# Sparse attention in units of two batches, with tiled scores and routing lists built on the chip

## The chip, the core and the metric

The kernel runs on one core of a Trainium2 chip. The core has a matrix engine (TensorE, PE in the profile; its weight loads are listed apart as PEld), a vector engine (VectorE, DVE), a scalar engine (ScalarE, ACT), a general engine (GpSimd, POOL) and a sequencer that mostly starts transfers (SyncE, SP). Each works through its own list of instructions in order and waits for the others on semaphores. Transfers between DRAM and the on-chip memory run on 16 DMA engines. TensorE writes to PSUM, a small memory of 8 banks; the other operands lie in SBUF.

The metric is the time of one execution on the device in microseconds (us).

## The reference

Block-sparse attention over 4 batches, 8 heads, 768 positions and 64 channels, and then a mixture of 8 experts, in which every token goes to at most one expert:

```python
mask = np.abs(blk_i - blk_j) <= 1
mask = mask | (blk_i == 0) | (blk_j == 0) | (blk_i == n_blocks - 1) | (blk_j == n_blocks - 1)
for qb in range(n_blocks):
    for kb in sampled_blocks[qb]:          # three per query block
        mask[qb * 32:(qb + 1) * 32, kb * 32:(kb + 1) * 32] = True
scores = np.where(mask, scale * q @ k.T, -1e9)
attn = softmax(scores); out = attn @ v     # (4, 8, 768, 64)
x = out as 3072 tokens of 512
do_compute = x @ w_skip > 0                # the others keep x
e_idx = argmax(x @ w_gate); gate = the softmax's value there
y = gate * (relu(x @ w1[e_idx]) @ w2[e_idx]); result = x + y
```

The 768 positions are 24 blocks of 32. Query blocks 0 and 23 look at all keys. Each of the other 22 looks at eight blocks of keys at most: blocks 0 and 23, its own and its two neighbours, and three sampled ones; so 256 keys.

## The kernel before, in words

The work has three stages in time.

**Dense units.** Query blocks 0 and 23 make 16 units (class `Dense`), one for each batch and pair of heads.

**Sparse units.** The other 22 query blocks make 88 units (class `Sparse`), one for each block and batch, in the order of the blocks. A unit has 8 heads of 32 queries, that is 256 rows of scores of 256 keys, and runs through six steps:

- `S`: scores on TensorE, four matmuls of 256 columns (L401). The channels of two heads lie one above the other in the 128 partitions. The queries of such a pair are laid out with zeros (64 columns: 32 of the one head with zeros in the lower half, 32 of the other with zeros in the upper half), so one matmul over all 128 partitions gives the scores of both heads. Two such matmuls go to different halves of the output's partitions.
- `M`: row maxima on VectorE (L409), and a second small instruction that scales and negates them (L410).
- `X`: exponentials on ScalarE, two of 256 columns (L416), with the score's scale in the instruction.
- `T`: four transposes of 128x128 on TensorE (L421).
- `V`: ScalarE copies the transposed 512 columns from PSUM to SBUF (L425).
- `A`: 16 matmuls of 65 columns on TensorE (L435), each on a strip of 32 of the array's columns, four strips in turn; the 65th column sums the row. `N` then divides on VectorE (L446, L447, L448).

An fp32 matmul is two records in the profile, a transpose one. The main loop (`for k in range(-LA, nu + 1)`) writes the steps of different units beside each other: in step k stand S and M of unit k+3, X of unit k+2, T of unit k+1, V and A of unit k, N of unit k-1. So TensorE's list is S, A, T, S, A, T without end.

The keys of a query block are gathered on the chip: `load_k` lets GpSimd copy them out of `kts`, which holds all keys, into `kg[0]` or `kg[1]` by the block's parity (two copies for the window, L187, and three for the sampled blocks, L202, as multiplications by a tile of ones). The values come by DMA from DRAM, five transfers of 260 KB for each block (`load_v`: two of the window, three sampled), and the queries in one of 512 KB (`load_q`). Key and value loads of block i+2 are issued behind the last unit of block i. Four transfers of 64 KB write a finished block to `out`.

**Routing lists.** After each group of three or four blocks (`BATCHES`), `route` works out which expert each token goes to and its place in that expert's list, in seven steps that the main loop takes one at a time (`fetch`). Its last act is a scatter by GpSimd, one per block: 128 entries of two numbers (token, gate) into the DRAM tensor `lst` (L73, out `lst`). `pick_first` and `look_first` choose, some units before the end, the expert with the most tokens so far, read its first 256 entries back from `lst`, and gather those tokens' rows.

**Experts.** If that first expert has its 256 tokens, its first matmuls (`gemm1` on `early["t"]`, L747 to L749) start at once behind the attention, and the routing of the last group is written between them (`beside`). Then `lists` reads all of `lst` by one transfer, `order_lists` puts the first expert in front, and eight experts follow, each with two matrix products in split precision. The weights of the first expert and half of those of the next (twelve transfers of 512 KB) overwrite `kts` when the last keys have been gathered.

## Time and profile before

| | |
|---|---|
| runs | 573.26, 575.48 (median), 579.07 us |
| the profiled execution | 573.99 us, span 572.3 us, granted TensorE clock 0.96 |
| TensorE busy | 499.7 us, 87% of the span |
| VectorE, ScalarE, GpSimd busy | 358.0, 250.8, 214.8 us |
| moved by DMA | 108.36 MB, 189 GB/s on average |
| first matmul of a sparse unit | at 56.74 us |
| first matmul of an expert | at 301.25 us |

The span is the time between the first and the last instruction. Busy time is the union of an engine's instructions. Several small matmuls can run in the array at once; their listed mean is the time of one from start to end, so mean times count is more than the busy time. "issue" stands where an engine waited for nothing that the profile shows. In the tables of stretches, the columns are the stretch, its length, the busy time and number of instructions of PE, PEld, DVE, ACT and POOL, then the granted clock, the share of time for which the DMA engines were busy, and GB/s.

### The profile page before, as it was taken

How to read it: one execution, taken by the hardware profiler on the slowest of the kernel's cores; microseconds unless marked ns; L12 is line 12 of the kernel's file. 1: busy time of each engine (PE TensorE's matmuls, PEld its weight loads, DVE VectorE, ACT ScalarE, POOL GpSimd, SP SyncE). 2: the span in 40 equal slices, each digit the busy share in tenths (PEclk: the TensorE clock that was granted, in tenths of full speed). 3: DMA queues.
4: the chain of work that ended last, by engine and by line, in shares of the span. 5: the costliest groups of instructions: out<-in, count | busy, mean ns of one | idle time of the engine just before them, and what ended most of it. 6: DMA issues, size and time to landing. Idle time of an engine off the chain costs nothing.

```text
span 572.3 us, 16047 instructions
## 1 busy us (share of the span) xinstructions
PE 499.7 (87%) x5842; PEld 369.4 (65%) x5842; DVE 358.0 (63%) x1028; ACT 250.8 (44%) x576; POOL 214.8 (38%) x236
## 2 busy tenths in 40 slices
PE   6999999899899799799877976989999977899980
PEld 4777765466566466465456755978797854777970
DVE  4877677678668578688667616656649573482510
ACT  3444555365355365454552205536354535361300
POOL 2008345736636636637436332150413240512020
PEclk9999999899799899999989979999999989999995
DMA  8999989967969879868996531564544564811010
GB/s 287 345 317 223 225 217 271 235 165 213 233 158 221 199 182 224 218 161 219 255 316 206 197 129 33 182 211 168 195 173 155 197 199 177 296 70 45 3 43 13
DMA packets 49565, 108.36 MB, mean 189 GB/s; under 512 B 7175, under 2 KB 35208, under 8 KB 43842
## 3 DMA queue, kind: packets, MB, share of 16 engines
q1 hardware_dynamic: 43760, 84.69, 53.9%
q0 software_dynamic: 5008, 20.69, 10.7%
q8 instruction: 70, 1.15, 1.0%
q14 instruction: 149, 1.22, 0.7%
q10 hardware_dynamic: 578, 0.61, 0.3%
HBM read 96.34 MB, written 12.30 MB: 190 GB/s over the span
## 4 chain that ended last, share of the span: by engine, by line
PE 43%; issue 27%; DVE 12%; DMA 8%; POOL 4%; SPq 1%; POOLq 1%; ACT 1%; DVEq 0%; ACTq 0%
PE sp L401 11%; PE op L435 7%; PE tp L421 7%; DMA x<-out,lt 6%; PE op L357 4%; PE sp L322 3%; DVE m L409 3%; DVE m L410 2%; PE tp L345 2%; POOL out L73 2%; POOL x L577 2%; DVE xs L448 1%; PE hp L749 1%; PE hp L747 1%; DMA kts<-kt 1%
## 5 line engine op out<-in xcount | busy, mean ns | idle before, releaser
L401 PE MATMUL sp<-kg,q 128*64 128x256 f32 x704 | 100.5, 405 | 1.6 <-issue 1.6
L425 ACT COPY pt<-tp 128x512 f32<-128x512 f32 x88 | 51.7, 587 | 107.5 <-PE tp L421 94.9
L409 DVE TENSOR_REDUCE m<-sp 128x2 f32<-128x512 f32 x88 | 60.2, 684 | 39.9 <-PE sp L401 32.1
L202 POOL TENSOR_TENSOR kg<-kts,onesf 128x512 f32<-128x512 f32 x66 | 82.1, 1274 | 0.1
L73 POOL DMA_INDIRECT out<-o,lt x17 | 18.8, 1104 | 153.7 <-DVE o L830 153.4
L187 POOL TENSOR_SCALAR kg<-kts 128x512 f32<-128x512 f32 x50 | 30.0, 621 | 121.4 <-PE sp L401 82.5
L416 ACT ACTIVATE pr<-sp,m 128x256 f32<-128x256 f32 x176 | 74.2, 478 | 2.8 <-DVE rs L446 2.8
L747 PE MATMUL hp<-xh,w1h 128*128 128x256 f32 (+3 forms) x192 | 59.5, 310 | 14.6 <-DVE o L830 7.5
L401 PEld LDWEIGHTS sp<-kg,q 128*64 128x64 f32 x704 | 44.9, 140 | 34.7 <-issue 22.1
L421 PE MATMUL tp<-ident,pr 128*128 128x128 f32 x352 | 60.4, 292 | 4.2 <-issue 4.1
L752 ACT ACTIVATE hh<-hp 128x256 fp32r<-128x256 f32 (+2 forms) x56 | 21.3, 383 | 85.7 <-PE hp L749 63.0
L748 PE MATMUL hp<-xl,w1h 128*128 128x256 f32 (+3 forms) x192 | 58.9, 307 | 0.0
L749 PE MATMUL hp<-xh,w1l 128*128 128x256 f32 (+3 forms) x192 | 58.8, 306 | 0.0
L435 PEld LDWEIGHTS op<-va,pt 128*32 128x32 f32 x1376 | 31.3, 110 | 42.4 <-ACT pt L425 23.2
L755 DVE SCALAR_TENSOR_TENSOR hl<-hp,hh 128x256 fp32r<-128x256 f32 (+2 forms) x56 | 23.2, 416 | 50.8 <-ACT hh L752 19.7
L435 PE MATMUL op<-va,pt 128*32 128x65 f32 x1376 | 48.3, 228 | 7.5 <-issue 2.2
L435 PE MATMUL op<-vb,pt 128*32 128x65 f32 x1376 | 49.0, 223 | 6.6 <-issue 6.6
L747 PEld LDWEIGHTS hp<-xh,w1h 128*128 128x128 f32 x192 | 37.3, 194 | 17.7 <-issue 15.4
L421 PEld LDWEIGHTS tp<-ident,pr 128*128 128x128 f32 x352 | 38.1, 143 | 12.8 <-issue 5.0
L813 PE MATMUL yp<-w2h,hh 128*128 128x512 f32 x112 | 45.4, 405 | 0.0
L814 PE MATMUL yp<-w2l,hh 128*128 128x512 f32 x112 | 45.0, 402 | 0.1
L815 PE MATMUL yp<-w2h,hl 128*128 128x512 f32 x112 | 44.7, 399 | 0.0
(209 smaller groups left out, 983.7 us busy)
## 6 DMA issues: line engine op xcount, KB each, us to landing
vb<-v SPq DMA_DIRECT2D x68, 260.0 KB
va<-v SPq DMA_DIRECT2D x48, 260.0 KB
kts<-w SPq DMA_DIRECT2D x6, 2048.0 KB
kts<-w POOLq DMA_DIRECT2D x6, 2048.0 KB
q<-qs SPq DMA_DIRECT2D x22, 512.0 KB
vt<-v SPq DMA_DIRECT2D x16, 390.0 KB
kts<-w SPq DMA_DIRECT2D x12, 512.0 KB
kts<-kt SPq DMA_DIRECT2D x15, 384.0 KB
```

Source lines behind the costliest of these rows:

```text
L202: nc.gpsimd.tensor_tensor(out=kg[x][:, :, c0:c0 + BS], in0=kts[:, :, bass.ds(kr * BS, BS)], in1=onesf[:, 0:BS].unsqueeze(1).broadcast_to([ ...
L401: nc.tensor.matmul(out=self.sp[64 * j:64 * j + 64, g, :], lhsT=qt[self.i][:, p, :], rhs=kg[self.x][:, p, :], start=True, stop=True)
L409: lambda: nc.vector.reduce_max(out=self.mx, in_=self.sp, axis=AX.X),
L416: nc.scalar.activation(out=self.pr[:, g, :], in_=self.sp[:, g, :], func=AF.Exp, bias=self.mx[:, g:g + 1], scale=SCALE)
L421: nc.tensor.transpose(out=self.tp[:, u, :], in_=self.pr[:, u // 2, (u % 2) * P:(u % 2) * P + P], identity=ident)
L425: nc.scalar.copy(out=self.pt, in_=self.tp)
L435: nc.tensor.matmul(out=self.op[32 * hh:32 * hh + 32, g, :], lhsT=self.pt[:, 2 * g + t, 32 * hh:32 * hh + 32], rhs=vt[:, 8 * self.b + 4 * g ...
L747: nc.tensor.matmul(out=hp[:, 0:w], lhsT=wh[:, f, k, :], rhs=xh[:, k, 0:w], start=(k == 0), stop=False)
L748: nc.tensor.matmul(out=hp[:, 0:w], lhsT=wh[:, f, k, :], rhs=xl[:, k, 0:w], start=False, stop=False)
L749: nc.tensor.matmul(out=hp[:, 0:w], lhsT=wl[:, f, k, :], rhs=xh[:, k, 0:w], start=False, stop=(k == NK1 - 1))
L813: nc.tensor.matmul(out=yp, lhsT=hh[:, f, cs], rhs=wh[:, f, :], start=(f == 0), stop=False)
L814: nc.tensor.matmul(out=yp, lhsT=hh[:, f, cs], rhs=wl[:, f, :], start=False, stop=False)
```

## The change

It touches the sparse stage and the lists; the dense units and the experts are as before but for the layout of heads and the places from which lists are read.

- **Units of two batches.** 44 sparse units in place of 88. A unit holds two batches' 512 rows: twice the exponentials, transposes, copies and value matmuls of a unit before.
- **Tiled scores.** Queries come without zeros (`qs` is half as large). A head's score matmul takes its 64 channels alone, in the upper or the lower half of the array's rows, and its 32 queries go to one strip of 32 columns. A unit has 16 such matmuls of 256 columns, the two heads of a pair in turn; heads of the upper half go to the PSUM tile `sp0`, those of the lower half to `sp1`.
- **The scale goes to the queries.** GpSimd multiplies each block's queries by 0.125 when they have landed; the reduction for the maxima negates, and the small instruction behind it is gone.
- **Keys copied plainly.** All copies are `tensor_copy`.
- **Two courses.** The blocks are taken in the order 1, 12, 2, 13, ... 11, 22 (`ORDER`); blocks 1 to 11 use the first store of keys and values, blocks 12 to 22 the second. Since a store sees neighbours one after another, only one new block of its window has to be fetched: one key copy in place of two, four value transfers in place of five.
- **Lists on the chip.** A token's place is turned into a row of 128 zeros and a one (`rows_of_ones`) and its two numbers into a row of 24 columns each (`entries`); a matmul of the two adds the group's tokens into a table in PSUM (`put`), and VectorE adds that to `lsf`. No scatter to `lst` and no reading back are left, outside a branch for experts of more than 384 tokens. `route` has 13 steps in place of 7, and the last group has four blocks in place of two.
- **Other places.** The loop counts in `q`, two for each sparse unit; the twelve weight loads are issued one at each q from 14 before the end (before: two, two, and then one at each step from 10 before the end). The filling of later rows of `out` is spread over eight small transfers.

The inner changes of the diff:

```diff
+ORDER = [i for pair in zip(range(1, HALF), range(HALF, NB - 1)) for i in pair]
+BATCHES = [[0, NB - 1] + ORDER[:2]] + [ORDER[a:b] for a, b in ((2, 6), (6, 9), (9, 12), (12, 15), (15, 18), (18, 22))]
...
     def window(i):
-        return (i - 1, i, i + 1) if i <= 2 else (i, i + 1)
+        return (i - 1, i, i + 1) if i in ORDER[:2] else (i + 1,)
...
         for r, c0 in enumerate((64, 96, 224)):
             kr = nc.gpsimd.value_load(kidx[0:1, i, r:r + 1], min_val=0, max_val=NB - 1)
-            nc.gpsimd.tensor_tensor(out=kg[x][:, :, c0:c0 + BS], in0=kts[:, :, bass.ds(kr * BS, BS)],
-                                    in1=onesf[:, 0:BS].unsqueeze(1).broadcast_to([P, NPAIR, BS]), op=ALU.mult)
+            nc.gpsimd.tensor_copy(out=kg[x][:, :, c0:c0 + BS], in_=kts[:, :, bass.ds(kr * BS, BS)])
+
+        nc.gpsimd.tensor_scalar(out=qt[i], in0=qt[i], scalar1=SCALE, scalar2=0.0, op0=ALU.mult, op1=ALU.add)
...
         def S(self):
-            self.sp = ps_s.tile([P, 2, 256], F32, name="sp")
+            self.sp = [ps_s.tile([P, 2, 256], F32, name=f"sp{w}") for w in range(2)]
             for g in range(2):
-                for j in range(2):
-                    p = 4 * b + 2 * g + j
-                    nc.tensor.matmul(out=self.sp[64 * j:64 * j + 64, g, :], lhsT=qt[self.i][:, p, :], rhs=kg[self.x][:, p, :], start=True, stop=True)
+                for a in range(4):
+                    p = 4 * (self.b + g) + a
+                    for w in range(2):
+                        ws = slice(64 * w, 64 * w + 64)
+                        nc.tensor.matmul(out=self.sp[w][32 * a:32 * a + 32, g], lhsT=qt[self.i][ws, p, :], rhs=kg[self.x][ws, p, :], start=True, stop=True)
...
         def M(self):
-                lambda: nc.vector.reduce_max(out=self.mx, in_=self.sp, axis=AX.X),
-                lambda: nc.vector.tensor_single_scalar(out=self.mx, in_=self.mx, scalar=-SCALE, op=ALU.mult),
+            return [lambda w=w: nc.vector.tensor_reduce(out=self.mx[:, w], in_=self.sp[w], axis=AX.X, op=ALU.max, negate=True) for w in range(2)]
...
-        def scatter():
-            for t in range(T):
-                scatter_to(
-                    out=lst[:, :], out_offset=bass.IndirectOffsetOnAxis(ap=st["adr"][:, t:t + 1], axis=0),
-                    in_=st["pay"][:, t, :], in_offset=None, bounds_check=P * E * LC - 1, oob_is_err=False)
+        def put():
+            st["lp"] = ps_r.tile([P, 2, E * CS], F32, name="rps")
+            for t in range(T):
+                nc.tensor.matmul(out=st["lp"], lhsT=st["plo"][:, t], rhs=st["phi"][:, t], start=(t == 0), stop=(t == T - 1))
+        d6 = [
+            lambda: V.tensor_tensor(out=lsf, in0=lsf, in1=st["lp"], op=ALU.add),
...
+    def sparse_step(k):
+        q = nd + 2 * (k - nd) if k >= nd else k
+        if fresh:
+            units[k + 2].S()
+        mix(units[k - 1].N(), [])
+        pe, soon, then, pool = work(q)
+        mix(soon, [])
+        if k + 1 < nu:
+            units[k + 1].T()
+            units[k + 1].V(0)
+        if pe is not None:
+            pe()
+        flush()
+        if k < nu:
+            units[k].A()
+        if fresh:
+            mix(units[k + 2].M(), [])
+        if k + 2 < nu:
+            units[k + 2].X()
+        if k + 1 < nu:
+            units[k + 1].V(1)
...
+            pe, soon, then, pool = work(q + 1)
```

TensorE's list in the middle of the sparse stage, before, from one unit's scores to the next unit's: sp are scores, op the products with the values va and vb, tp the transposes.

```order
L401 MATMUL sp<-kg_89,q 64x256 x4
L435 MATMUL op<-va_90,pt 32x65 x4
L435 MATMUL op<-vb_92,pt 32x65 x4
L435 MATMUL op<-va_90,pt 32x65 x4
L435 MATMUL op<-vb_92,pt 32x65 x4
L421 MATMUL tp<-ident,pr 128x128 x4
```

The same place in the changed kernel, from the last pair of a unit's scores (seven such pairs stand ahead of it):

```order
L429 MATMUL sp_1466<-kg_85,q 32x256
L429 MATMUL sp_1467<-kg_85,q 32x256
L449 MATMUL tp<-ident,pr 128x128 x8
L468 MATMUL op<-va_88,pt 32x65 x4
L468 MATMUL op<-vb_90,pt 32x65 x4
L468 MATMUL op<-va_88,pt 32x65 x4
L468 MATMUL op<-vb_90,pt 32x65 x4
```

Two more such pairs of op rows end the unit. Scores now come as 16 matmuls of 32 columns of queries in turn to two tiles; the transposes of the next unit have moved ahead of this unit's value products; and the array changes from one shape of work to another three times for two batches, where it did so six times.

GpSimd's list at a block's key gather before, where it follows a group's scatter:

```order
L73 DMA lst<-pay,adr 26624x2 x4
L187 TENSOR_SCALAR kg_89<-kts 128x16x32 x2
L201 TENSOR_LOAD kidx
L201 ISA x2
L202 ISA
L202 TENSOR_TENSOR kg_89<-kts,onesf 128x16x32
```

And in the changed kernel, behind the scaling of the block before:

```order
L214 TENSOR_SCALAR q<-q 128x512
L192 COPY kg_85<-kts 128x16x32
L211 TENSOR_LOAD kidx
L211 ISA x2
L212 ISA
L212 COPY kg_85<-kts 128x16x32
```

The last four rows of either piece stand three times for a block (once shown). The scatter is gone, the window takes one copy, and the scaling of the queries, which waits for their transfer, stands at the end of each gather.

VectorE's list between two units before: the maxima of one unit, then the division of another.

```order
L409 TENSOR_REDUCE m_2469<-sp 128x2
L410 TENSOR_SCALAR m_2469<-m_2469 128x2
L446 TENSOR_SCALAR rs<-op 128x2
L447 RECIPROCAL rs<-rs 128x2
L448 TENSOR_TENSOR xs<-op,rs 128x128
```

In the changed kernel, at a place where two steps of the list building stand between (col, phi and lsb are the rows of ones that `put` multiplies):

```order
L479 TENSOR_SCALAR rs<-op 128x4
L480 RECIPROCAL rs<-rs 128x4
L481 TENSOR_TENSOR xs<-op,rs 128x256
L315 TENSOR_TENSOR col<-cols,cols_of 128x96
L311 TENSOR_TENSOR phi<-col,pays 128x192
L436 TENSOR_REDUCE m_2327<-sp_2190 128x2
L436 TENSOR_REDUCE m_2327<-sp_2191 128x2
L307 TENSOR_TENSOR lsb<-pos,rows_of 128x512
```

The division comes once for two batches, the small instruction behind the maxima is gone, and steps of the lists stand ahead of a unit's maxima.

## The prediction

> **What bounds the kernel now.** I read the page first, then busy times by stretches: the sparse stage lies between the first scores of a sparse unit, at 56.74, and the first expert matmul, at 301.25.

> ```profile
> PE 499.7 (87%) x5842; PEld 369.4 (65%) x5842; DVE 358.0 (63%) x1028; ACT 250.8 (44%) x576; POOL 214.8 (38%) x236
> ...
> 56.74 1.08 PE L401 MATMUL sp<-kg,q 128*64 128x256 f32 x8
> 301.25 0.36 PE L747 MATMUL hp<-xeh,w1h 128*128 128x256 f32 x1 [0.36 <-DVE ohs L288]
> ...
> 20.00:40.00 20.00, 20.00 (x201) 15.24 (x199) 16.64 (x67) 8.48 (x19) 0.00 (x0) 1.00 1.09 334
> 60.00:292.00 232.00, 211.36 (x3876) 133.42 (x3876) 167.80 (x585) 119.69 (x274) 124.22 (x127) 0.97 0.86 213
> 301.25:572.30 271.05, 225.01 (x1302) 190.00 (x1302) 141.12 (x270) 98.90 (x236) 70.21 (x71) 0.95 0.41 141
> ```

> The stage takes 244.5 of 572.3 us. TensorE is busy for 211 of the 232 us in its middle; the DMA engines, with a share of 0.86, come next. In this stretch run about 44 pairs of units, so 5.27 us for two batches. The timeline of TensorE's rows shows an undisturbed unit, from scores to scores, and the chain of waits has the same shapes in the dense stage:

> ```profile
> 102.73 1.08 PE L401 MATMUL sp<-kg,q 128*64 128x256 f32 x8
> 103.75 0.32 PE L435 MATMUL op<-va,pt 128*32 128x65 f32 x8
> 104.34 0.66 PE L421 MATMUL tp<-ident,pr 128*128 128x128 f32 x4
> 104.92 1.08 PE L401 MATMUL sp<-kg,q 128*64 128x256 f32 x8
> ...
> 11.37 1.29 PE sp L322 x4
> 12.66 1.36 PE op L357 x24
> 132.29 1.00 PE rps L239 x8
> ```

> From start to start: scores 1.02, value products 0.59, transposes 0.58, together 2.19; two batches cost 4.38. In the dense rows nothing runs side by side: a record of 65 columns takes 1.36/24 = 0.057 us, one of 384 takes 1.29/4 = 0.32, so one of 256 takes 0.215. A sparse unit's 8 score records would take 1.72 one by one and take 1.02: two side by side (0.86) and 0.16 to turn over to the next shape. Its 32 value records would take 1.82 and take 0.59: four side by side (0.46) and 0.13. Transposes: 0.11 each and 0.15. A group's routing adds 1.0 us (L239) and about 0.8 for its small matmuls; six groups over 44 pairs are 0.25, which makes 4.63. Measured is 5.27. The missing 0.64, 28 us in all, lies in a few places, such as this one (PE rows, then POOL rows):

> ```profile
> 104.92 1.08 PE L401 MATMUL sp<-kg,q 128*64 128x256 f32 x8
> 106.52 0.32 PE L435 MATMUL op<-va,pt 128*32 128x65 f32 x8 [0.51 <-issue]
> ...
> 108.07 0.34 PE L435 MATMUL op<-vb,pt 128*32 128x65 f32 x7 [0.96 <-issue]
> 108.84 0.31 PE L421 MATMUL tp<-ident,pr 128*128 128x128 f32 x1 [0.43 <-issue]
> 109.58 0.27 PE L421 MATMUL tp<-ident,pr 128*128 128x128 f32 x1 [0.42 <-issue]
> 110.97 1.91 PE sp L401 x8
> ...
> 104.48 1.20 POOL L73 DMA_INDIRECT lst<-pay,adr  x1 [2.68 <-DVE adr L293]
> 108.52 0.97 POOL L73 DMA_INDIRECT lst<-pay,adr  x1 [0.30 <-issue]
> ```

> While GpSimd issues a group's scatters, TensorE stops and starts without a wait that shows, and the next scores run at half pace (1.91 for 1.02): this unit took 6.05 us and the next one 3.4, some 5 us lost. The chain shows two more such slow scores (152.56, 196.77), each just behind a scatter; five groups fall into the stretch, 5 x 5 = 25 of the 28 us. So but for the scatters, TensorE's own work sets the pace.

> ```profile
> 152.56 1.99 PE sp L401 x7
> 196.77 1.91 PE sp L401 x8
> ...
> 150.65 0.97 POOL L73 DMA_INDIRECT lst<-pay,adr  x1 [0.30 <-issue]
> 193.46 0.97 POOL L73 DMA_INDIRECT lst<-pay,adr  x1 [0.30 <-issue]
> ```

> **The change, part by part**, for one new unit (two batches). *Transposes and value products* keep their number, with one turn-over where there were two: 8 x 0.11 + 0.15 = 1.03, and 64 records, four side by side, 16 x 0.057 + 0.13 = 1.04. *Scores*: 32 records of 256 columns in place of 16, each on half the rows and a quarter of the columns, so up to eight fit side by side: 4 x 0.215 + 0.16 = 1.02 (before 2.04). If only the four strips run side by side, 8 x 0.215 + 0.16 = 1.88; if nothing does, 32 x 0.215 + 0.16 = 7.04. No row of before has two row halves at work; the nearest are the value products, where four tiles overlap fully though each tile's two records follow each other in the list, so I take 1.02. [...] *Lists*: as now, and one `put` for a group (eight records of 48 columns, about 0.5 us), 2.3 us x 6 over 42 steps = 0.33. TensorE: 1.03 + 1.04 + 1.02 + 0.33 = 3.42.

> The others, from the 232 us row divided by 44 and these groups (lines grouped; busy us and mean ns of one):

> ```profile
> L409 DVE TENSOR_REDUCE m<-sp 128x2 f32<-128x512 f32 x88 | 60.2, 684 | 39.9 <-PE sp L401 32.1 <-remote 5.8 <-ACT pr L416 1.7
> L410 DVE TENSOR_SCALAR m<-m 128x2 f32<-128x2 f32 x88 | 35.4, 403 | 3.0
> L448 DVE TENSOR_TENSOR xs<-op,rs 128x128 f32<-128x128 f32 x86 | 25.1, 291 | 3.8 <-DMA out<-xs 0.4 <-DVE rs L447 0.4
> L447 DVE RECIPROCAL rs<-rs 128x2 f32<-128x2 f32 x88 | 14.6, 166 | 3.0
> L446 DVE TENSOR_SCALAR rs<-op 128x2 f32<-128x2 f32 x86 | 13.4, 156 | 13.2 <-PE tp L421 8.2 <-PE op L435 2.3 <-PE sp L401 1.6
> L202 POOL TENSOR_TENSOR kg<-kts,onesf 128x512 f32<-128x512 f32 x66 | 82.1, 1274 | 0.1
> L187 POOL TENSOR_SCALAR kg<-kts 128x512 f32<-128x512 f32 x50 | 30.0, 621 | 121.4 <-PE sp L401 82.5 <-DMA vt<-v 37.7 <-remote 1.1
> L425 ACT COPY pt<-tp 128x512 f32<-128x512 f32 x88 | 51.7, 587 | 107.5 <-PE tp L421 94.9 <-remote 4.3 <-PE sp L401 3.4
> vb<-v SPq DMA_DIRECT2D x68, 260.0 KB
> q<-qs SPq DMA_DIRECT2D x22, 512.0 KB
> out<-xs SPq DMA_DIRECT2D x88, 64.0 KB
> ```

> - VectorE: 167.8/44 = 3.81. L410 goes (35.4/44 = 0.80), half of L446 and L447 goes (28.0/88 = 0.32), a division of 256 for two of 128 saves some 0.16, the lists add about 1.2 us for a group (one operation of 512 elements like L409, two shorter), 0.17 a step: 2.70.
> - ScalarE: 119.69/44 = 2.72; the shapes of its exponentials and copies stay, so it stays.
> - GpSimd: 124.22/44 = 2.82. The three random copies of a block fall from 1.27 to about 0.62 if a plain copy costs what L187 does (bounds 0.3 to 1.27; hidden either way), one window copy makes room for the scaling, the scatters go (about 0.45): 1.4. The scaling waits for the queries with nothing behind it but the next gather, and S of that block comes three steps later.
> - DMA, by bytes of a block: 5 x 260 + 512 + 4 x 64 = 2068 KB before, 4 x 260 + 256 + 256 = 1552 KB now, 0.75 of it. Busy 0.86 x 5.27 = 4.53 for two batches before, 3.40 now. Values have three steps less the products to land, 3 x 3.65 - 1.0 = 9.9 us, where they had 5 x 2.63 - 0.6 = 12.6.

> So TensorE (3.42) and DMA (3.40) stand level, the others at 2.7. Before, the pace without scatters was TensorE's sum; the dense stage ran TensorE without a gap at a DMA share of 1.09 (20 to 40 us). With two equal loads I add 0.23 of waiting: 3.65 a step.

> **The sum.** The first sparse scores stay at 56.7. Two steps with dense work beside them take 3.25 each as now and one without scores some 2.2: 65.4. Then 42 steps have scores: 42 x 3.65 = 153.3, to 218.7. The rest (T and A of the last units 3.1, the early rows' transposes 1.2, copies between them 2.2, and 2.5 because the splitting of the first weights and twelve weight loads now share 7 long steps) makes 9: the first expert matmul at 227.7 in place of 301.25, 73.5 us earlier. The weight loads move ahead of the last block's values on SP's queue; at 213 GB/s four of them are 9.8 us and those values 5.0 more, against about 10 of cover, so 0 to 5 us, of which the 2.5 is my share. Were that cover gone, the last two units would wait the 5.

> Behind 301.25 I change nothing:

> ```profile
> 306.81 0.44 PE L248 MATMUL rps<-ident,lsb 128*128 128x128 f32 x2 [1.60 <-ACT lsb L242]
> 325.10 1.03 POOL L577 DMA_INDIRECT x<-out,lt  x1 [7.15 <-DVE lt L858]
> lt<-lst SPq DMA_DIRECT2D x1, 208.0 KB
> ```

> The 1.6 us lie beside scatters (302 to 305.7) and may go; the last group has four blocks in place of two, so about 1.5 more on TensorE between the expert's matmuls. The list's transfer goes, but the gathers at 325.1 wait for VectorE's list in its order, and that order is the same. Between 3 us less and 3 more; I take 0. Profiled execution 573.99 - 73.5 = 500.5; the median stands 1.5 above it: **502 us**.

> **Rivals.**

> 1. *Bound by transfers or by the reading of PSUM.* If the DMA share can't rise above the 0.86 of now, a step is 3.40/0.86 = 3.95: 42 x 0.30 = 12.6 more, 515. If VectorE's 3.81 did not shrink (its small operations stretched, as L410's mean of 403 beside L446's 156 shows), a step is about 4.05, 519. For it: the sums are level and the cover of the values is shorter; against: no product in the stage waits for values now. [...] Together 0.20.
> 2. *Half the overlap.* Only four strips side by side: TensorE 4.28, step 4.4, 42 x 0.75 = 31.5 more, 533. 0.15.
> 3. *No overlap, slower than before.* If the two row halves exclude each other and, as the list alternates between them, nothing overlaps, scores take 7.04, a step 9.44: 42 x 5.79 = 243 more, 745. It turns slower from a step of 3.65 + 73.5/42 = 5.4, that is scores of 2.8, fewer than 2.6 records side by side. 0.04.
> 4. *The change doesn't do what it says:* if the first expert lacks 256 tokens among the fewer blocks that are done by then (17 of 24), the list building stands ahead of its matmuls, some 24 us (301.25 to 325.1): 526. The reference's arithmetic on its inputs gives that expert 297; 0.01.

> The forecast itself has 0.60, between a step of 3.42 with 3 us gained behind (42 x 0.23 = 9.7, 489) and 3.9 (513). The range goes from 487, a little below that floor, to 537, the second rival with 0.1 a step more. A measurement of this kernel can tell about 1% from no change, 5.8 us. Faster: all but the third rival and a small rest, 0.95; within 1%: 0.01; slower 0.04.

> **What would show it.** In the middle of the stage score rows of 16 matmuls that start within about 1.0 us (1.9 is the second rival, 7 the third); units 3.5 to 3.8 us apart, with no gaps marked "issue" of the kind above and no scores at half pace; the first expert matmul near 228; TensorE busy about 440 us in all; a DMA share near 0.9. Value products that wait for a transfer, or maxima that start over 1 us behind the scores, mean the first rival. If the units come at 3.65 and the time still isn't near 500, what I left unchanged behind the first expert matmul is wrong.

## The result, and the profile after

The changed kernel takes 534.45 us (median of 6 runs, 528.81 to 538.21), the kernel before 575.9 in the same series: a ratio of 0.924 (95% interval 0.917 to 0.931). That is 41.5 us less, faster as forecast and inside the range (487 to 537), but at its far end: 73.5 us were worked out. The profiled execution is the slowest of the six, 538.21 us with a span of 536.5; it counts as a slow run and is left out of the ratio.

The busy times by stretches of the changed kernel: the middle of the sparse stage, up to the last scores; then the last 19.55 us ahead of the first expert matmul; then all that follows. Columns: stretch, length, TensorE, its weight loads, VectorE, ScalarE, GpSimd, granted clock, DMA share, GB/s. Ahead of it stands the page's own sum over the span.

```profile
PE 457.1 (85%) x6594; PEld 358.0 (67%) x6594; DVE 315.6 (59%) x818; ACT 246.4 (46%) x576; POOL 151.6 (28%) x215
```

```profile
66.00:238.00 172.00, 154.91 (x4442) 111.09 (x4448) 117.76 (x368) 109.86 (x264) 60.59 (x98) 0.96 0.82 203
242.65:262.20 19.55, 7.47 (x148) 6.17 (x146) 8.13 (x23) 5.15 (x10) 9.28 (x8) 0.68 1.00 301
262.20:536.50 274.30, 229.44 (x1315) 193.83 (x1315) 139.69 (x267) 99.93 (x236) 62.12 (x63) 0.93 0.38 134
```

The first expert matmul starts at 262.20: 39 us earlier than before (301.25), but 34.5 later than the forecast's 227.7. Behind it run 274.3 us (before 271.05), so nearly all of the miss lies in the stage. The chain of waits shows an undisturbed step and, further on, a disturbed one:

```profile
92.14 1.05 PE op L468 x64
93.19 1.02 PE sp L429 x32
94.21 1.02 PE tp L449 x8
95.23 1.05 PE op L468 x64
96.28 1.02 PE sp L429 x32
...
160.85 1.00 PE sp L429 x27
161.86 3.44 issue
165.30 1.07 PE sp L429 x5
166.37 1.90 PE tp L449 x8
168.26 1.89 PE op L468 x64
```

From scores to scores the undisturbed step takes 3.09 us, to the hundredth what was worked out (1.02 + 1.03 + 1.04). But from the third scores (67.41) to the last (237.61) 41 steps take 4.15 on average, in place of 3.65. TensorE stops in the middle of its scores, 27 records in and 5 to go, for 3.44 us and with no wait that the profile shows; then it goes on at half pace. The granted clock says so too (1.00 ahead of this stop, 0.53 behind it):

```profile
158.00:161.80 3.80, 3.69 (x110) 2.56 (x104) 3.24 (x14) 2.53 (x6) 0.00 (x0) 1.00 1.01 253
165.30:171.70 6.40, 6.40 (x109) 4.13 (x108) 3.40 (x8) 2.53 (x6) 3.07 (x5) 0.53 0.53 129
```

The second part of the miss is the end of the stage, in the timeline (TensorE's rows, then SyncE's transfers):

```profile
242.63 0.19 PE L274 MATMUL rps<-oh,ones 128*128 128x16 bf16 x2
249.85 0.45 PE L468 MATMUL op<-va,pt 128*32 128x65 f32 x8 [7.03 <-DMA va<-v]
260.92 1.49 PE L325 MATMUL rps<-phi,lsb 128*128 128x48 f32 x6 [3.05 <-DVE lsb L307]
262.20 0.56 PE L841 MATMUL hp<-xeh,w1h 128*128 128x256 f32 x1
...
234.55 1.86 SPq L522 DMA_DIRECT2D kts<-w  x2
237.66 1.44 SPq L232 DMA_DIRECT2D va<-v  x2
240.99 1.49 SPq L522 DMA_DIRECT2D kts<-w  x2
```

The last block's values are issued at 237.66, behind four weight transfers, and land 12 us later; TensorE stands still for 7.03 us, and the granted clock, 0.68 on average over these 19.55 us, is 0.5 from 246.47 to 256.71.

What are the stops? The list of DMA queues has two for instructions. Between 66 and 238 us they moved (packets, MB, share)

```profile
q8 instruction: 35, 0.57, 1.5%
q14 instruction: 12, 0.10, 0.2%
```

Queue q8 brought 35 packets of 16 KB, one every 4.87 us; TensorE executed 8,890 records (4442 matmuls, 4448 weight loads) in that time, about 250 for each packet. So I take a packet of q8 for a page of some 250 TensorE instructions; the kernel before gives the same count (7,752 records and 31 packets between 60 and 292). Against these packets stand six of the 20 stops of TensorE of over 0.5 us, from matmul start to matmul start (read from the trace; us):

```
stop            length   page's packet ended   stop ended behind it by
 79.35- 81.79    2.44          80.43                 1.36
108.17-109.33    1.16         107.89                 1.44
131.52-133.56    2.05         132.07                 1.50
161.48-165.30    3.82         163.95                 1.35
207.58-208.99    1.41         207.30                 1.69
217.77-218.79    1.02         217.38                 1.41
```

Of all 20 stops between 66 and 238, which take 23.1 us, 17 with 21.4 us end 1.35 to 1.69 us behind a page; the other three are 0.5 to 0.6 us long, two of them in the half-pace stretches. If the stops fell anywhere in the 4.87 us between two pages, one in fourteen would. So TensorE seems to run out of instructions; that is a reading of these times, since the profile shows no wait there.

### The profile page after: what moved, and what is told of

It is laid out like the page before. It is cut to its first block, busy times and chain, and to the rows that moved or that the text cites. A ratio compares the mean times of both kernels' runs of the same rounds, so it can differ in the third digit from the quotient of the medians.

```text
span 536.5 us, 17078 instructions
## 1 busy us (share of the span) xinstructions
PE 457.1 (85%) x6594; PEld 358.0 (67%) x6594; DVE 315.6 (59%) x818; ACT 246.4 (46%) x576; POOL 151.6 (28%) x215
## 3 DMA queue, kind: packets, MB, share of 16 engines
q0 software_dynamic: 4208, 20.67, 11.1%
q8 instruction: 76, 1.25, 1.1%
## 4 chain that ended last, share of the span: by engine, by line
PE 46%; issue 28%; DMA 11%; POOL 5%; DVE 4%; ACT 1%; SPq 1%; POOLq 1%; DVEq 0%; ACTq 0%
PE sp L429 9%; PE op L468 8%; PE tp L449 8%; DMA x<-out,lt 7%; PE op L383 4%; PE sp L349 4%; PE tp L371 2%; POOL out L73 2%; DMA va<-v 2%; POOL x L619 2%; PE hp L841 1%; PE hp L843 1%; PE hp L842 1%; DMA out<-xs 1%; PE rps L325 1%
## 5 line engine op out<-in xcount | busy, mean ns | idle before, releaser
L436 DVE TENSOR_REDUCE m<-sp 128x2 f32<-128x512 f32 x88 | 56.6, 685 | 22.4 <-PE sp L429 21.0
L442 ACT ACTIVATE pr<-sp,m 128x256 f32<-128x256 f32 x176 | 69.1, 482 | 0.8 <-DVE m L436 0.8
L73 POOL DMA_INDIRECT out<-o,lt x17 | 18.7, 1102 | 159.0 <-DVE o L924 158.7
L429 PE MATMUL sp<-kg,q 64*32 64x256 f32 x1408 | 54.3, 393 | 7.3 <-issue 7.3
L449 PEld LDWEIGHTS tp<-ident,pr 128*128 128x128 f32 x352 | 39.2, 144 | 23.2 <-issue 12.1
L449 PE MATMUL tp<-ident,pr 128*128 128x128 f32 x352 | 50.6, 287 | 3.8 <-issue 3.0
L468 PE MATMUL op<-vb,pt 128*32 128x65 f32 x1376 | 47.5, 228 | 4.8 <-issue 3.8
L468 PEld LDWEIGHTS op<-va,pt 128*32 128x32 f32 x1376 | 34.2, 114 | 17.6 <-issue 17.3
L212 POOL COPY kg<-kts 128x512 f32 x66 | 41.1, 630 | 7.3 <-POOL kg L212 2.7
L468 PEld LDWEIGHTS op<-vb,pt 128*32 128x32 f32 x1376 | 35.6, 114 | 6.1 <-issue 6.1
L528 DVE TENSOR_TENSOR w2l<-kts,w2h 128x512 fp32r<-128x512 f32 x56 | 38.2, 686 | 1.5
## 6 DMA issues: line engine op xcount, KB each, us to landing
kts<-w SPq DMA_DIRECT2D x12, 512.0 KB, 5.4
```

The source lines that it names most:

```text
L429: nc.tensor.matmul(out=self.sp[w][32 * a:32 * a + 32, g], lhsT=qt[self.i][ws, p, :], rhs=kg[self.x][ws, p, :], start=True, stop=True)
L436: return [lambda w=w: nc.vector.tensor_reduce(out=self.mx[:, w], in_=self.sp[w], axis=AX.X, op=ALU.max, negate=True) for w in range(2)]
L442: nc.scalar.activation(out=self.pr[:, g, w], in_=self.sp[w][:, g], func=AF.Exp, bias=self.mx[:, w, g:g + 1])
L449: nc.tensor.transpose(out=tp[:, u, :], in_=self.pr[:, g, u // 2, (u % 2) * P:(u % 2) * P + P], identity=ident)
L468: nc.tensor.matmul(out=self.op[32 * a:32 * a + 32, g, w, :], lhsT=self.pt[:, g, 2 * w + t, 32 * a:32 * a + 32], rhs=vt[:, 8 * (self.b + g) ...
```

## The experiments

Theory: pages of TensorE's instructions arrive late, because the new step uses them faster (208 instructions in 3.4 us, before 176 in 4.6) and the kernel's data stand ahead of them. Rivals: the stops come from other engines' work; or each page takes its time whatever else moves. For the end of the stage: late values, against weights and list steps.

**Less data: values of the random blocks left out**

```diff
-        for r, dst in enumerate((va[x][64:96], va[x][96:128], vb[x][96:128])):
+        for r, dst in enumerate((va[x][64:96], va[x][96:128], vb[x][96:128]) if i in ORDER[:2] else ()):
```

> The changed kernel, but the values of the three random blocks are loaded only for the first block of each of the two courses (20 x 3 transfers of 260 KB are left out, the value products use old rows; instructions of TensorE stay the same, the data of a block falls from 1552 to 772 KB). In the changed kernel scores follow scores at 4.15 us on average, at 3.09 where nothing stops TensorE; its stops end about 1.5 us after a 16 KB page of its instructions has been moved by the DMA engines. Theory 1 (pages of instructions come late because data of the kernel fill the DMA engines): with half the data the stops go, units come at 3.4 to 3.5 us, the last scores start near 210 (now 237.6), the first expert matmul comes near 230 (now 262.2), the time is about 502. Theory 2 (pages come late by themselves: 208 instructions per step need a page every 4.9 us, and one page takes that long whatever else is moved): units stay at 4.1, only the wait for the last block's values goes, first expert matmul near 252, time about 525. Theory 3 (TensorE's stops come from the other engines' work): units stay above 4.0 too, and no stop is marked as issue.

Units came at 3.67 us, the last scores at 217.1 and the first expert matmul at 233.34 (without these values the routing differs, so what follows isn't comparable: 639.86 us in all). The stretch up to the last scores:

```profile
66.00:217.00 151.00, 143.56 (x4412) 104.30 (x4408) 118.34 (x365) 108.20 (x258) 63.46 (x100) 1.00 0.50 136
```

Ten stops with 10.2 us are left of 20 with 23.1, and 6.5 us of them end 1.3 to 1.5 us behind a page. With the same instructions, the same work on VectorE, ScalarE and GpSimd and half the data the step falls by 0.48 us and pages come more often (4.28 us for 4.87), so neither rival explains the stops. The theory had asked for more, 3.4 to 3.5 us and no stops: a page every 4.28 us is still late at times, and 3.7 of the 10.2 us end elsewhere than behind a page and stay unexplained.

**The scores on 128 rows: four side by side in place of eight**

```diff
-  ... lhsT=qt[self.i][ws, p, :], rhs=kg[self.x][ws, p, :] ...
+  ... lhsT=qt[self.i][:, p, :], rhs=kg[self.x][:, p, :] ...
```

> The changed kernel with the tiled scores on all 128 rows: the same 32 records, each over both row halves (the score is then the sum of two heads, which is not the reference's), so that only the four column strips can run side by side. By the working of the prediction scores take 1.88 in place of 1.02. Theory 1 (instruction pages late): TensorE is slower but needs its pages less often, so part of the stops goes: units at about 4.6 us in place of 4.15, first expert matmul 19 us later, about 281, time about 553. Rival (stops do not depend on how fast the instructions are used): units at 5.0, 36 us later, first expert matmul about 298, time about 570. If the eight-fold overlap were not what makes the scores 1.02, they stay at 1.02 and the time at 534.

The scores take 1.90 from start to start, so the row halves do run side by side in the changed kernel, fully. But the time is 537.51 us, and the first expert matmul comes at 262.87, 0.7 later:

```profile
151.76 1.97 PE L429 MATMUL sp<-kg,q 128*32 128x256 f32 x32
153.66 1.09 PE L449 MATMUL tp<-ident,pr 128*128 128x128 f32 x8
...
262.87 0.56 PE L841 MATMUL hp<-xeh,w1h 128*128 128x256 f32 x1
```

```profile
66.00:238.00 172.00, 171.90 (x4356) 130.24 (x4355) 115.41 (x359) 107.63 (x258) 60.37 (x98) 1.00 0.77 197
```

In this stretch TensorE is now busy for 171.90 of 172 us without a stop of over 0.5 us, and units come at 4.22. I had expected a part of the slowdown to be absorbed; nearly all of it was. With all the data moving, the second half of the overlap buys next to nothing (0.07 us a step).

**Both at once** (the two edits above together)

> Both at once: the values of the random blocks loaded only for the first block of each course, and the scores on all 128 rows (both leave the reference's result; read only up to the first expert matmul). With all values loaded, slower scores (1.90 in place of 1.02) changed the units only from 4.15 to 4.22 us. With fewer values and the eight-fold scores the units came at 3.67 us, last scores at 217.1, first expert matmul at 233.3. Theory (the tiling over row halves is worth its 0.86 us only where pages of instructions come in time): units at 4.2 to 4.25, which is TensorE's own time, no stops over 0.6 us, last scores near 241, so that the tiling is worth some 22 us with light data and 3 with full data. Rival (the shorter scores are hidden whatever the data): units at 3.7 to 3.8, last scores near 220.

Units at 4.21, last scores at 239.9, first expert matmul at 256.50, TensorE busy throughout at a DMA share of 0.43:

```profile
66.00:238.00 172.00, 171.66 (x4360) 130.21 (x4360) 117.30 (x361) 107.51 (x258) 61.90 (x99) 1.00 0.43 117
```

So the tiling over row halves is worth 0.54 us a step where data are few (4.21 against 3.67) and 0.07 where they are many (4.22 against 4.15). That it saves TensorE time is true in both; whether the step gets shorter depends on the data that move beside it, by the theory through the pages.

**Fewer, longer instructions**

```diff
-                    for w in range(2):
+                    for w in range(2) if g == 0 else ():
...
+                    if g == 1:
+                        r = 64 * (a % 2)
+                        nc.tensor.matmul(out=self.sp[a // 2][r:r + 64, g], lhsT=qt[self.i][:, p - p % 2:p - p % 2 + 2, :].rearrange("d a s -> d (a s)"),
+                                         rhs=kg[self.x][:, p, :], start=True, stop=True)
```

> The changed kernel with the scores of the second batch of each step as four matmuls of 128 rows by 64 columns in place of eight of 64 by 32 (its scores are then not the reference's): a step has 192 instructions of TensorE in place of 208, and TensorE's own time in a step rises from 3.42 to 3.9 (scores 4 x 0.215 + 2 x 0.215 + 0.16 = 1.45 in place of 1.02). Theory (a step can't be shorter than its share of the pages, some 5 us for 256 instructions; the stops are what is missing): no stops of more than 0.6 us, units at 3.9 to 4.0 us in place of 4.15, the last scores start near 230 in place of 237.6, although TensorE has more to do. Rival (the stops come on top of TensorE's own time): units at 4.6, the last scores near 257.

An undisturbed step takes 3.68 (before this edit 3.09), the units came at 4.03, the last scores at 235.2: 2.4 us earlier than in the changed kernel, although TensorE has 0.6 us more to do in each step. The profiled execution of the changed kernel held some 5 us at half pace, though; beside the kernel with only the first weights inside the stage (below), which held none there, it is a draw (4.08, last scores at 235.5). (What follows the first expert matmul isn't comparable here either.)

```profile
66.00:235.00 169.00, 167.76 (x4111) 113.74 (x4113) 120.73 (x367) 108.98 (x262) 62.10 (x101) 1.00 0.83 208
```

Four stops with 2.7 us are left. The theory's 5 us for 256 instructions agrees with the changed kernel's counts (254 records for a packet of q8, one packet every 4.87 us). The 4.6 of the rival is ruled out; there is next to no gain in itself, since TensorE's own 4.01 (3.68 and 0.33 for the lists) now sets the step.

The kernels side by side, from 66 us to the last scores (the kernel before from 60 to 292; its own step and the 0.33 for the lists in all the others are the prediction's):

```
                        TensorE's own   DMA     a page   stops over   measured
                        step (us)       share   every    0.5 us       step
changed kernel             3.42         0.82    4.87     20, 23.1     4.15
fewer values               3.42         0.50    4.28     10, 10.2     3.67
half wide scores           4.01         0.83    5.08      4,  2.7     4.03
scores on 128 rows         4.18         0.77    5.04      1,  0.8     4.22
both                       4.18         0.43    4.99      2,  1.2     4.21
first weights only         3.42         0.82    4.73     20, 23.4     4.08
kernel before              4.63         0.86    7.52     32, 31.0     5.44
```

With full data, a page every 5 us mostly comes in time in the new step; at 3.42 us a step of 208 instructions one would be wanted about every 4 us (an estimate, with the 250 records to a page counted above), and it doesn't come. The rate alone doesn't decide, though: in the kernel before, with a page every 7.52 us, 7 of the 32 stops (8.6 of 31.0 us, the longest of 2.93 us among them) also end 1.28 to 1.59 us behind a page. When a page is asked for isn't in the trace, so how long it takes was not measured. What holds a late one up was not shown either: the pieces of the values, 8320 bytes each, take 0.547 us in the changed kernel's trace (mean of 2501), and no run here shows in which order a DMA engine takes them and the packets of q8.

**The scatters of before**

```diff
-            for t in range(T):
+            for t in range(T) if len(tiles) == 2 else ():
                 scatter_to(
```

> The kernel before without the scatters of the first six groups' lists (only the last group's two are left; the lists of most tokens stay empty, so what follows the first expert matmul is not comparable). The prediction put 25 of 244.5 us down to these scatters: the first expert matmul comes 25 us earlier, near 276 in place of 301.25, and two batches at 4.7 us in place of 5.27. Rival (most stops are late instruction pages, which the scatters only worsen at two or three places): 10 to 14 us earlier, 287 to 291, and stops marked issue remain at other places.

```profile
60.00:273.00 213.00, 204.31 (x3883) 130.28 (x3881) 166.08 (x587) 120.84 (x275) 105.67 (x108) 1.00 0.92 228
```

```profile
282.50 0.36 PE L747 MATMUL hp<-xeh,w1h 128*128 128x256 f32 x1 [0.35 <-DVE ohs L288]
```

The first expert matmul comes 18.75 us earlier (282.50 for 301.25); two batches take 4.97 in place of 5.44 from the first to the last scores, TensorE is busy for 204 of 213 us. Between the two expectations: the five groups that fell into the stage cost 3.75 us each and not 5, and that is somewhat over half of what was missing there (0.47 of the 0.81 us between 5.44 and TensorE's 4.63). Stops marked issue remain, 19 with 14.1 us from 60 to 273, of which 5 with 5.5 us end 1.4 to 1.7 us behind a page. In size the 18.75 are close to half of the 39 us by which the changed kernel is ahead at this point.

**The weights behind the last values**

```diff
-        if -4 <= z < 8:
-            which, p = (("1", 0), ("2", 0), ("1", 1))[(z + 4) // 4]
-            load_w(which, p, z % 4, 4)
+        for y in range(2 * z, 2 * z + 2) if 0 <= z < 6 else ():
+            which, p = (("1", 0), ("2", 0), ("1", 1))[y // 4]
+            load_w(which, p, y % 4, 4)
```

> The changed kernel with the twelve first weight transfers issued only behind the transfers of the last block's values (two at each of six places from there, splitting of the first weights correspondingly later). Theory (these values wait behind weights: 7.0 us idle of TensorE, then half clock): the values land about 6 us after issue in place of 11, TensorE's wait of 7.0 us falls below 1, the first expert matmul comes at 250 to 254 in place of 262.2, the time falls by 8 to 10 us to about 525. Rival (what sets the end is the weights themselves and the list steps of the sixth group): the wait moves to the splitting of the first weights, the first expert matmul stays at 260 or later, the time stays at 532 to 538. Units before that stay at 4.15 us by both.

526.84 us (ratio 0.910, 0.902 to 0.919), some 8 us less; units stayed at 4.15. TensorE's wait for the values is gone; the first expert matmul comes at 257.71, less early than expected, because the next small transfer now stands behind the weights (VectorE's row):

```profile
249.93 0.42 DVE L481 TENSOR_TENSOR xs<-op,rs 128x256 f32<-128x256 f32 x1 [3.79 <-DMA out<-xs]
```

**Only the first weights inside the stage**

```diff
-        for y in range(2 * z, 2 * z + 2) if 0 <= z < 6 else ():
+        for y in {2: (0, 1), 3: (2, 3), 10: range(4, 12)}.get(z, ()):
```

> The changed kernel with only the first expert's first weights (four transfers of 512 KB) issued inside the stage, behind the last block's values and behind the output rows of the block before it; the other eight weight transfers follow the last output rows. Where the weights were only put behind the values, the first expert matmul came at 257.71, and VectorE still waited 3.79 us for output rows that stood behind weights. Theory (the end of the stage is set by small transfers that stand behind weights): that wait falls below 1 us, the first expert matmul comes near 250 to 253, the time is 518 to 523. Rival (the end is set by the list steps of the sixth group, or by the weights, which now come later): the first expert matmul at 257 or later, or the expert's second products wait for their weights, and the time is 526 or more.

523.67 us (ratio 0.905, 0.900 to 0.910), the fastest median of all kernels here that compute the reference, 11 us below the changed kernel (the intervals of this run and the last overlap). That wait is gone, and the first expert matmul starts at 250.91, behind the list steps of the sixth group, which are now the last thing:

```profile
249.64 1.48 PE L325 MATMUL rps<-phi,lsb 128*128 128x48 f32 x6 [3.53 <-DVE lsb L307]
250.91 0.56 PE L841 MATMUL hp<-xeh,w1h 128*128 128x256 f32 x1
```

Units came at 4.08 with as many stops as ever (20, 23.4 us) but no half-pace stretch up to the last scores (granted clock 1.00). Half pace cost the profiled execution of the changed kernel some 5 us: seven pieces in three places, such as the 1.90, 1.89 and 1.62 that follow 161.86, where 1.02 to 1.05 are usual.

**Smoother data: values in halves, then other queues (both failed)**

```diff
-            if self.b == 2 and next_of(self.i):
-                load_v(next_of(self.i))
+            if next_of(self.i):
+                load_v(next_of(self.i), (self.b // 2,))
```

> The kernel with only the first expert's first weights inside the stage (523.67 us, units at 4.08 us, last scores at 235.5, first expert matmul at 250.91), and each block's values now loaded in two halves of 16 heads, the first half as soon as the value products of the block's first unit in that course are done: the same bytes in packets of 4160 in place of 8320 bytes, spread over both steps instead of in one burst of 1 MB. Theory (the pages of instructions are late because they stand behind bursts of big packets): fewer and shorter stops, units at 3.7 to 3.9 us, last scores at 221 to 229, first expert matmul at 236 to 244, time 509 to 517. Rival (it is the amount of data alone, or the page's own time): units stay at 4.0 to 4.15, time at 520 to 526; were the twice as many issues on the queue too many for it, units above 4.3 and 532 or more.

593.49 us (ratio 1.037, 1.019 to 1.056): units at 5.5. SyncE's queue has no room for it. Some of its transfers over one block (start, duration; the next block's first stands 11.92 us behind this one's):

```profile
151.36 0.39 SPq L232 DMA_DIRECT2D vb<-v  x1
152.56 1.47 SPq L235 DMA_DIRECT2D va<-v  x2
154.82 0.32 SPq L235 DMA_DIRECT2D vb<-v  x1
...
160.11 1.81 SPq L492 DMA_DIRECT2D out<-xs  x4
163.28 0.38 SPq L232 DMA_DIRECT2D vb<-v  x1
```

One half's four transfers take 3.8 us, since ahead of each random block its number is read into a register (0.8 us, as between 151.75 and 152.56). Two halves, the output rows, the queries and the rows of ones fill some 11 of the 11.9 us. TensorE's longest stops (up to 5.1 us) fall on value products and mostly end 2 to 8 us behind a page, not 1.5: they are marked issue too, so that mark alone doesn't say page.

The next edit, on the kernel with only the first weights inside the stage, moves transfers to another queue:

```diff
-        nc.sync.dma_start(out=qt[i], in_=qs[i])
+        nc.scalar.dma_start(out=qt[i], in_=qs[i])
...
-                ins = nc.sync.dma_start(out=out3[:, BS * i ...
+                ins = (nc.scalar if hh < 2 else nc.sync).dma_start(out=out3[:, BS * i ...
```

> The kernel with only the first expert's first weights inside the stage (523.67 us, units at 4.08), with each block's queries and two of its four output transfers issued by ScalarE in place of SyncE. It takes 0.55 + 2 x 0.45 = 1.45 us per block off a queue that issues for some 6.8 of 8.2 us. If SyncE's queue doesn't bound the stage, nothing changes but ScalarE's sum (2.72 + 0.33 + 0.7 = 3.8 of 4.1): units 4.0 to 4.2, time 520 to 528. If transfers that were held up on that queue cost something: units at 3.8, time near 512.

551.96 us (ratio 0.952, 0.945 to 0.959), units at 4.7: 28 us slower than without this edit, which I had not expected. Value products now wait for their transfers by the profile's own account:

```profile
PE op L468 <- DMA va<-v: 10.9, 6, 6.2
PE op L468 <- DMA vb<-v: 6.4, 6, 2.2
```

(us in all, times, longest; up to 236 us). SyncE issues them late: two transfers that take it 1.47 us in the other kernel take 3.81 and 4.13 at 148.00 and 138.81. What holds it there stands among SyncE's own waits:

```profile
SPq L232 <- DMA out<-xs: 24.0, 10, 3.9
SPq L229 <- DMA q<-qs: 19.2, 7, 4.2
```

A transfer of values (L229, L232) needs neither output rows nor queries. But in the trace a transfer waits for the semaphore on which it will signal its own landing, and that semaphore may have been given to a transfer of the other queue before. So the second of the two at 148.00 starts at 151.49, 0.02 us after ScalarE's output transfer of 146.96 has landed: both carry semaphore 104. 16 of these 17 waits end like this, 0.02 us after a transfer of ScalarE with the same semaphore. In the kernel with everything on SyncE no transfer of values waits for queries or output rows. The slowdown thus comes, at least in good part, from waits that the program put between the two queues, and not from a want of room on either.

And both, with the halves' registers read once:

```diff
+            if h == 0:
+                vregs[i, r] = nc.sync.value_load(vidx[0:1, i, r:r + 1], min_val=0, max_val=NB)
+            vr = vregs[i, r]
```

> The same, and each block's values in two halves of 16 heads, spread over the two steps, with the block numbers read into registers only once. Where this was tried with everything on SyncE's queue, that queue issued for 11.1 us of every 11.9 per block, and the value products waited for values that were issued too late. Here it has 3.8 + 1.5 + 0.9 = 6.2 us of issuing per block. Theory (pages of instructions are late because they stand behind bursts of big packets): fewer and shorter stops than with whole transfers, units at 3.7 to 3.9, time 508 to 517. Rival (the amount of data alone makes pages late): units at 4.0 to 4.15 and time as with whole transfers, within 4 us. Should a queue or ScalarE bound it, units above 4.3 and 530 or more, with idle time of TensorE that does not end 1.5 us after a page.

577.72 us (ratio 0.995, 0.990 to 0.999), units at 5.1, TensorE stopped on value products again (25.3 us marked issue, up to 4.6 us at once). SyncE's transfers of values waited for queries and output rows here too (24.8 us up to 236). Both runs with halves were held up by SyncE, by its issuing or by its waits, before they could say anything on bursts: few stops end 1.25 to 1.75 us behind a page in them (2 with 1.1 us up to 286, 3 with 3.6 us up to 236), but a page is wanted only every 6 to 7 us. Whether pages are late because of the amount of data, the bursts or the size of their packets stays open.

## Why the prediction was right, and where its sum was wrong

- *The time within the range: luck in good part.* The forecast itself (489 to 513, with a chance of 0.60) failed by 21 us. The range holds 534.45 only because it was drawn up to the second rival's 533, and that rival did not come true. Three of its own signs failed too: 20 stops marked issue where none were to be, units at 4.15 in place of 3.5 to 3.8, TensorE busy for 457 in place of 440 us.
- *Scores, eight side by side: right* (1.02; transposes 1.02, value products 1.05, each within a hundredth). The second and third rivals are out. Eight records overlap fully here, 6.88/(1.02 - 0.16) = 8.0 times, with the 0.16 of turning over as worked out ahead.
- *The 0.23 of waiting a step: the term that failed.* Measured is 0.73 (4.15 - 3.42); over 42 steps the 0.50 more are 21.0 of the 34.5 us. It was taken as friction between two level loads, TensorE and DMA. The runs show a coupling: where the second load is halved (DMA share 0.50 for 0.82), TensorE's stops halve (10.2 for 23.1 us), and by their timing behind the pages it is the first one's instructions that come late. Had 176 instructions in 4.6 us been set against 208 in 3.4, the row of the instruction queue would have asked the question.
- *Scatters, 25 of 28 us: the scatters do cost time, but 18.75 us.* What was missing was mis-sized as well: the 232 us held 42.7 pairs of units and not 44, so two batches took 5.44 and not 5.27, and 0.81 a pair was missing and not 0.64, some 35 us in all. Late pages, which the prediction didn't know of, were part of the rest (8.6 of the 31.0 us of stops end 1.28 to 1.59 us behind one). So "but for the scatters, TensorE's own work sets the pace" was wrong before the change already (4.97 without them, for 4.63).
- *First rival (DMA share at most 0.86, step 3.95):* its arithmetic comes close, 3.40/0.82 = 4.15, but not by its mechanism. Inside the stage no value product waits for a transfer, and with shares of 0.77 and 0.43 alike the step is 4.2 once TensorE's own time is that long. VectorE and ScalarE (117.76 and 109.86 of 172 us) bound nothing.
- *The end of the stage, 9 us with 2.5 for the weights moved ahead of the last values: mis-sized.* It took about 20.5 (from 241.7, where the 42 steps end, to 262.20). "0 to 5" was worked out from the bytes ahead of the values alone. The values, the clock that fell while TensorE waited (0.5 from 246.47 to 256.71), and output rows behind the same weights come to about 9.2 of the 11.5 too much: in the run with only the first weights inside, the same end takes 11.3 (from 239.6 to 250.91). The other 2.3 were not traced.
- *The start of the 42 steps* came 2.0 us later than worked out (67.41 for 65.4).
- *Nothing behind the first expert matmul: right within its bounds, nearly.* 274.3 for 271.05, where 3 were allowed. The same part took 268.9 in the run with the weights behind the values and 274.9 in the one with only the first weights inside, so 3 us either way may be the place of the weights or the difference between executions; no run separates them.
- *GpSimd's plain copies:* 630 ns for the 620 assumed, hidden as said. *SyncE's queue* wasn't in the sum at all. It had room here, but none with each block's values in halves.

Sum of the miss in the profiled execution: 2.0 + 21.0 (some 5 of them at half pace) + 11.5 at the end + 3.3 behind = 37.8, and 500.5 + 37.8 = 538.3, for 538.21 measured. The median lies 3.8 below that execution, and so 32.5 above the forecast.

## What to carry to other kernels

Many small matmuls have a price that isn't in TensorE's busy time: count instructions, divide by the 250 or so that went with a packet of q8 here, and see how often a page is wanted, above all while data fill the DMA engines (stops of 23.1 us at a share of 0.82, of 10.2 at 0.50); in this step one in 5 us mostly came in time (2.7 us of stops at one in 5.08) and one in 4, as estimated, did not, and in the kernel before even one in 7.52 was late at times. Before shortening a step on one engine, make that engine slower in an experiment: if nothing gets slower, something else sets the pace. Bulk transfers whose result is needed late go behind the small ones that the next products wait for, on the queue and in the program (here weights ahead of values held TensorE up for 7.03 us). When transfers are spread over two queues, read the waits of the engine that issues them: here one queue came to wait for the other's transfers (43.2 us for queries and output rows).

## What the runs showed of the hardware

```profile
161.13:164.55 3.42, 0.73 (x27) 0.17 (x12) 0.98 (x6) 0.46 (x1) 0.62 (x1) 1.00 1.09 247
79.21:82.63 3.42, 1.36 (x32) 0.96 (x13) 1.79 (x4) 0.84 (x3) 2.44 (x4) 1.00 0.93 210
164.55:171.38 6.83, 6.08 (x103) 4.13 (x108) 3.26 (x8) 2.53 (x6) 3.07 (x5) 0.50 0.58 135
```

The length of a stop alone doesn't decide: the clock dropped behind the one of 2.05 us (131.52) and not behind one of 2.37 us in the kernel before (272.35; granted clock 1.00 up to 291.19). What makes it drop was not shown.

- Matmuls of 64 rows by 32 columns run eight at a time without a loss that shows (32 records of 256 columns take 1.02 us up to the next shape of work); on 128 rows the same records take 1.90.
- Moving 1.45 us of issuing per block from SyncE to ScalarE made the kernel 28 us slower: SyncE's transfers of values then waited 43.2 us, up to 4.2 us at once, for ScalarE's queries and for output rows, with which they shared semaphores.
